# Attention and gate: products in four column strips instead of two row halves, scores in bursts

## The chip, the cores and the metric

One NeuronCore of a Trainium2 chip runs the whole kernel in one launch. The metric is the device time in microseconds. Its engines are TensorE (PE in the profile; PEld is its weight load), VectorE (DVE), ScalarE (ACT), GpSimd (POOL) and SyncE (SP), which issues most of the DMAs.

## The reference

x is 2048 x 640, one batch; attention has 32 heads of 20 columns; the dense layer has 1536 hidden columns. All inputs are float32.

```python
xn = _layernorm(x)                                # over the 640 columns
qkv = xn @ wqkv                                   # 640 x 1920
p = softmax(q @ k.T * 20 ** -0.5)                 # 32 heads, 2048 x 2048 each
s = (p @ v) @ wo
h = maximum(xn @ w1, 0)                           # 2048 x 1536
g = silu(h @ w2)
return x + s * g
```

## The kernel before

**Arithmetic.** The scores, the weighing of the values by the exponentials, and the dense products all run on TensorE. The dense ones ("products": projections of q, k and v, hidden layer, gate, output) are done with float16 pairs: each operand is split into a high and a low part, and a sum over k tiles of 128 rows has three terms a tile (`terms`: high by high, high by low, low by high). A product is 512 columns wide (q, k, hidden; 15 terms a sum) or 320 wide (values 15, gate 36, output 12 or 3 terms).

**Attention.** It walks 8 groups of 4 heads, 4 chunks of 512 queries and 16 tiles of 128 keys: 512 steps. For a step, four scores (`st`, line 732: keys by queries, 62 rows) go to ScalarE, which writes their exponentials to `pt` (line 736). Four more scores (`mx`, line 629: queries by keys, 60 rows) go to VectorE, which takes their maxima (line 633); these belong to a coming chunk and end up as rows subtracted inside the `st` scores. When a step's four exponentials are there, `weigh` (line 772) multiplies them with the values into the bank `pv`: four matmuls at once, each in a strip of 32 columns of the array (21 in use). They are float32 and stand in the profile as two matmuls each, eight a step.

**Forms of the array.** A score has at most 62 rows, so two scores run at once, one in each half of the rows (form "A", 64 rows by 128 columns). The values run in four strips (form "P", 128 rows by 32 columns). Transposes and some products run in the full array (form "F"). A product in `products` (line 314) runs in form "A": two sums at once, each with half of its rows, then the other halves, after the first ones are known to be done. At the start and for the last steps `whole` (line 328) does it in form "F".

**Banks.** Of eight PSUM banks one is `pv`; the other seven (`banks`) go round between scores, products and transposes. `take` gives the bank that comes free first; a bank is held until the engine that empties it is done.

**The order.** A planner in the program's own Python (class `Plan`, and the loop at the end) writes out the order of all instructions while the kernel is built; on the chip each engine does them in that order, with semaphores between engines. The planner keeps the time at which each engine comes free by fixed costs (MM 216 ns, MM_HALF 136, PAIR 220, PV 850, EXP 585, RED 605, SWITCH for a change of form). At each turn it takes the first that can be had: a pair of scores (`pair`: st with mx, or two of a kind) if its banks are free within STAY (60 ns) and the engine that gets it has less than SOON (560 ns) of work left, or less than FULL (1300 ns) if the array is in form "A" already; else weighing; else small transposes; else work of the start (`first`), else a step of the products (`fill`, kept from running too far ahead by `pace`). A step of a product is one term of the two sums' halves.

Of the kernel before, what the change touches and what calls it, by code (L numbers as in the profile page):

```python
# [17 lines left out]
P = 128  # L18
# [5 lines left out]
KD = D // P  # L24
KF = DFF // P
NT = S // P
CW = 512
# [21 lines left out]
EPS = 1e-5  # L49


SWITCH = 100
LAG = 210
BACK = 120
PAIR = 220
# [17 lines left out]
MIXED = 400  # L73
STOCK = 900
AHEAD = 40000
OTS = 4
FILLING = NT * 15 * MM_HALF * 2 + (KD - 1) * NC * 30 * MM + NC * KF * 15 * MM + NT * 72 * MM_HALF
LEAD = 80
# [79 lines left out]
def attention_gate(ctx: ExitStack, tc: tile.TileContext, x, wqkv, wo, w1, w2, out):  # L158
# [136 lines left out]
            res += [(ah[:, k, sa], bh[:, k, sb]), (ah[:, k, sa], bl[:, k, sb]), (al[:, k, sa], bh[:, k, sb])]  # L295
        return res

    def products(ps, pairs, free):

        if st_done[0] == 0 or st_done[0] > 4 * (STEPS - 10):
            return (yield from whole(ps, pairs, free))
        cost = MM if ps[0].shape[-1] == CW else MM_HALF
        half = [slice(0, P // 2), slice(P // 2, P)]
        n = len(pairs[0])
        for second in range(2):
            for i in range(n):
                yield free  # L310
                for which in range(2):
                    rows = half[which ^ second]
                    a, b = pairs[which][i]
                    nc.tensor.matmul(ps[which], a[rows], b[rows],  # L314
                                     start=(i == 0 and not second), stop=(i == n - 1 and bool(second)))
                got = plan.pe("A", cost, free)
            if not second:
                last = plan.issued
                yield from when(lambda: plan.seen > last)
        return got  # L320

    def whole(ps, pairs, free):

        cost = MM if ps[0].shape[-1] == CW else MM_HALF
        for which in range(2):
            for i, (a, b) in enumerate(pairs[which]):
                yield free
                nc.tensor.matmul(ps[which], a, b, start=(i == 0), stop=(i == len(pairs[which]) - 1))
                got = plan.pe("F", cost, free)
        return got  # L330

    def take_two():
        (a, fa), (b, fb) = take(), take()
# [131 lines left out]
    def qk(m, c):  # L465

        cs = slice(c * CW, (c + 1) * CW)
        sc = SQ / (SX * SW)
        yield from when(lambda: ("q", m) in pieces and ("k", m) in pieces and c in turned)
        ws, at = zip(*(pieces[name, m] for name in "qk"))  # L470
        bs, free = take_two()
        got = yield from products([banks[b] for b in bs], [terms(w, xt, KD, slice(0, P), cs) for w in ws],
                                  max(free, xt_ready[c], *at))
        for name, b in zip("qk", bs):
            hi = stage.tile([P, CW], F16, name=f"hi{name}{m}{c}", tag="hi")
            lo = stage.tile([P, CW], F16, name=f"lo{name}{m}{c}", tag="lo")
            nc.scalar.mul(hi, banks[b], sc)
            done = plan.op("act", 480, got)
            r = stage.tile([P, CW], F32, name=f"r{name}{m}{c}", tag="r", bufs=2)
            nc.scalar.mul(r, banks[b], sc)  # L480
            bank_free[b] = done = plan.op("act", 480, got)
            nc.gpsimd.tensor_sub(lo, r, hi)  # L482
            done = plan.op("pool", 1160, done)

            plan.at(done, lambda name=name, hi=hi, lo=lo: store(name, m, c, hi, lo))

    pack_ready = {}

# [97 lines left out]
    def v_tiles(n, t):  # L586

        yield from when(lambda: ("v", n) in pieces and t // TPC in turned)
        w, ready = pieces["v", n]
        bs, free = take_two()  # L590
        got = yield from products([banks[b][:, 0:HD] for b in bs],
                                  [terms(xt, w, KD, slice(u * P, (u + 1) * P), slice(0, HD)) for u in (t, t + 1)],
                                  max(free, ready, xt_ready[t // TPC]))
        for u, b in zip((t, t + 1), bs):
            nc.scalar.mul(va[n][:, u, :, 0:DH], banks[b][:, 0:HD].rearrange("p (h d) -> p h d", d=DH), v_scale[n])
            bank_free[b] = v_ready[n, u] = plan.op("act", 410, got)

# [246 lines left out]
    def gate_hidden():  # L846
# [34 lines left out]
        for f in range(KF):  # L881
            fs = slice(f * P, (f + 1) * P)
            yield from when(lambda: ("1", f) in pieces)
            w, ready = pieces["1", f]
            for pr in range(NC // 2):
                two = [slice(c * CW, (c + 1) * CW) for c in (2 * pr, 2 * pr + 1)]
                bs, free = take_two()
                got = yield from products([banks[b] for b in bs], [terms(w, xt, KD, slice(0, P), cs) for cs in two],
                                          max(free, ready))
                for c, cs, b in zip((2 * pr, 2 * pr + 1), two, bs):  # L890
                    r = stage.tile([P, CW], F32, name=f"hr{c}{f}", tag="r", bufs=2)
                    hi = stage.tile([P, CW], F16, name=f"hh{c}{f}", tag="hi")
                    lo = stage.tile([P, CW], F16, name=f"hl{c}{f}", tag="lo")
                    nc.scalar.activation(r, banks[b], AF.Relu, scale=SH / (SX * SW))  # L894
                    bank_free[b] = done = plan.op("act", 480, got)
                    nc.gpsimd.tensor_copy(hi, r)  # L896
                    plan.op("pool", 610, done)
                    nc.gpsimd.tensor_sub(lo, r, hi)  # L898
                    done = plan.op("pool", 1160)

                    def store(fs=fs, cs=cs, f=f, c=c, hi=hi, lo=lo):
                        nc.sync.dma_start(h_d["h"][fs, cs], hi)
                        nc.sync.dma_start(h_d["l"][fs, cs], lo)
                        h_stored[f, c] = plan.arrival(2 * 2 * P * CW, 2)

                    plan.at(done, store)
                if pr == 0 and f + 2 < KF:
                    piece("1", w1, f + 2, P)
        yield from when(lambda: all(("w2", n) in h_stored for n in range(KF))
# [7 lines left out]
    def gate_out():  # L917
# [46 lines left out]
        for c in range(S // HW):  # L964
# [3 lines left out]
            for u in range(HW // P):  # L968
                t = c * (HW // P) + u
                gt = gp.tile([P, D], F32, name=f"g{t}", tag="g")  # L970
                bs, free = take_two()
                got = yield from products([banks[b][:, 0:HD] for b in bs],
                                          [terms(ht, w2t, KF, slice(u * P, (u + 1) * P), ns) for ns in halves],
                                          max(free, ready))
                for n, (b, ns) in enumerate(zip(bs, halves)):
                    ps = banks[b][:, 0:HD]
                    th = gp.tile([P, HD], F32, name=f"th{t}{n}", tag="th")
                    nc.scalar.activation(th, ps, AF.Tanh, scale=cz)
                    done = plan.op("act", 420, got)
                    nc.vector.scalar_tensor_tensor(gt[:, ns], th, 1.0, ps, op0=ALU.add, op1=ALU.mult)  # L980
                    bank_free[b] = done = plan.op("dve", 430, done)

                def store(t=t, gt=gt):
                    nc.sync.dma_start(g_d[t * P:(t + 1) * P, :], gt)
                    g_stored[t] = plan.arrival(4 * P * D)

                plan.at(done, store)
        yield from when(lambda: len(g_stored) == NT and KD - 1 in wo_ready)
        st.close()
        cs_o = const.tile([P, 1], F32, name="cs_o")  # L990
# [28 lines left out]
    def out_first():  # L1019
# [16 lines left out]
        for t in range(NT):  # L1036
            if t + 1 < NT:
                os_[t + 1] = yield from transposed(t + 1, ots[t + 1], KL, landed[t + 1], "f")
            o, ready = os_.pop(t)
            bs, free = take_two()  # L1040
            got = yield from products([banks[b][:, 0:HD] for b in bs],
                                      [terms(o, wot, KL, slice(0, P), ns) for ns in halves],
                                      max(free, ready, out_state["ready"]))
            for b, ns in zip(bs, halves):
                ps = banks[b][:, 0:HD]
                nc.vector.scalar_tensor_tensor(gts[t][:, ns], ps, cs_o, gts[t][:, ns], op0=ALU.mult, op1=ALU.mult)  # L1046
                bank_free[b] = done = plan.op("dve", 550, max(got, landed[t]))
                nc.gpsimd.tensor_add(pre[:, t, ns], pre[:, t, ns], gts[t][:, ns])  # L1048
                plan.op("pool", 880, done)
            pre_done[0] = t + 1  # L1050
            if t + OTS < NT:
                yield from when(lambda: (NG - 2, (t + OTS) // TPC) in o_stored)
# [2 lines left out]
    def out_rest(c, on, ready):  # L1055
# [9 lines left out]
        for i in range(TPC):  # L1065
# [1 line left out]
            gt = gts[i]  # L1067
            ot = o[0][:, i:i + 1, :], o[1][:, i:i + 1, :]
            ws = [w[:, KL:KD, :] for w in wot]
            bs, free = take_two()  # L1070
            got = yield from whole([banks[b][:, 0:HD] for b in bs],
                                      [terms(ot, ws, 1, slice(0, P), ns) for ns in halves], max(free, ready))
            for n, (b, ns) in enumerate(zip(bs, halves)):
                ps = banks[b][:, 0:HD]
                nc.vector.scalar_tensor_tensor(gt[:, ns], ps, cs_o, gt[:, ns], op0=ALU.mult, op1=ALU.mult)  # L1075
                bank_free[b] = done = plan.op("dve", 550, max(got, landed))
                if n and c + 1 == NC:
# [2 lines left out]
                else:  # L1080
                    nc.gpsimd.tensor_add(gt[:, ns], gt[:, ns], pre[:, t, ns])
                    done = plan.op("pool", 880, done)
            plan.at(done, lambda t=t, gt=gt: nc.sync.dma_start(out[t * P:(t + 1) * P, :], gt))


    first = deque()
# [165 lines left out]
    while True:  # L1252
# [2 lines left out]
        go = plan.begin("A", 0)  # L1255
        options = choose(t)
        inside = plan.mode == "A"
        now = [o for o in options if o[0] <= go + STAY and o[1] < (FULL if inside else SOON)]
        if now:
            best = min(now, key=lambda o: (o[1] if len(set(o[2])) == 1 else o[1] - MIXED))  # L1260
            pair(best[2])
# [65 lines left out]
```

## Time and profile before

| what | value |
|---|---|
| time, median of 2 runs | 1789.01 us (1787.75 to 1790.27) |
| the profiled execution's own time | 1788.3 us |
| its span, from first to last instruction | 1786.5 us |
| mean granted clock of TensorE | 0.992 |
| busy: PE, DVE, ACT, POOL | 1734.0, 1451.6, 1390.6, 315.9 us |
| matmuls: in all, scores, values, products in halves | 14887, 4096, 4096, 5844 |

A row of the page's groups reads: line, engine, operation, what it writes and reads, shapes, count, then busy time, mean length of one in ns, and the idle time of the engine before these, with what ended most of it. A row of the timeline reads: start, length, engine, line, operation, and how many were merged into it. A row of busy times by stretch reads: the stretch, its length, then busy time and count for each engine that has any, the granted clock, the DMAs' share and GB/s. A matmul's listed length is its whole way through the array, while the next one follows closer; the distance between starts is what it costs.

### The profile page before, as it was taken

What the parts mean: (1) busy time and instruction counts of PE and PEld (TensorE: products, weight loads), DVE (VectorE), ACT (ScalarE), POOL (GpSimd) and SP (SyncE); (2) the same over time, 40 slices, a digit from 0 to 9 for tenths busy, and PEclk for the clock granted to TensorE, in tenths of its full rate; (3) what the DMA queues carried; (4) which work ended last, traced back from release to release, by engine and by line L of the source; (5) the groups of instructions that cost most, each with busy time, mean ns of one, the idle gap of its engine ahead of it and who ended that gap; (6) DMA issues with size and microseconds to landing.
All of it is one profiled execution on the core that took longest, in us unless ns stands there. A gap on an engine that the chain in (4) does not pass through costs nothing. (4 is left out here: it accounts for less than half of the span.)

```text
span 1786.5 us, 36686 instructions
## 1 busy us (share of the span) xinstructions
PE 1734.0 (97%) x14887; PEld 723.6 (41%) x14887; DVE 1451.6 (81%) x2512; ACT 1390.6 (78%) x2338; POOL 315.9 (18%) x338
## 2 busy tenths in 40 slices
PE   4999999999999999999999989999999999999998
PEld 3443334444332333444433324444444444344332
DVE  7699988888888888888888878888888888887522
ACT  3537788888888888887887868888788878887785
POOL 1631200002111455322221103000000000012221
PEclk8999999999999999999999999999999999999998
DMA  6324311201115332311112071131013100323332
GB/s 240 102 62 125 99 33 35 49 20 37 58 41 162 96 93 89 107 51 43 45 39 73 29 216 42 55 92 56 13 55 92 55 9 20 109 87 124 102 100 74
DMA packets 133995, 135.30 MB, mean 76 GB/s; under 512 B 26640, under 2 KB 110480, under 8 KB 133824
## 3 DMA queue, kind: packets, MB, share of 16 engines
q1 hardware_dynamic: 133248, 131.63, 24.4%
q8 instruction: 116, 1.90, 0.4%
q10 hardware_dynamic: 576, 1.31, 0.2%
q14 instruction: 55, 0.45, 0.1%
HBM read 85.32 MB, written 47.58 MB: 74 GB/s over the span
## 5 line engine op out<-in xcount | busy, mean ns | idle before, releaser
L736 ACT ACTIVATE pt<-ps,cexp 128x512 f32<-128x512 f32 x2048 | 1249.4, 689 | 293.0 <-PE ps L732 244.8
L633 DVE TENSOR_REDUCE m<-ps 128x1 f32<-128x512 f32 x2048 | 1274.4, 684 | 211.0 <-PE ps L629 204.6
L629 PE MATMUL ps<-kp,qp 60*128 60x512 f16 x2048 | 585.6, 378 | 5.3 <-ACT pt L736 3.7
L732 PE MATMUL ps<-qp,kp 62*128 62x512 f16 x2048 | 579.4, 379 | 9.3 <-DVE m L633 4.7
L772 PE MATMUL pv<-pt,va 128*21 128x512 f32 x4096 | 523.0, 600 | 0.0
L732 PEld LDWEIGHTS <-kp 62*128 62x128 f16 x2048 | 147.3, 93 | 332.2 <-issue 289.6
L629 PEld LDWEIGHTS <-qp 60*128 60x128 f16 x2048 | 150.1, 93 | 117.3 <-issue 84.7
L772 PEld LDWEIGHTS pv<-pt,va 128*21 128x21 f32 x4096 | 88.4, 100 | 237.3 <-issue 226.4
L1048 POOL TENSOR_TENSOR pre<-pre,go 128x320 f32<-128x320 f32 x32 | 27.0, 864 | 596.3 <-DVE go L1046 596.3
L314 PE MATMUL ps<-w2th,hh 64*128 64x320 f16 x768 | 126.5, 296 | 0.1
L314 PE MATMUL ps<-w2th,hl 64*128 64x320 f16 x768 | 126.0, 295 | 0.0
L314 PE MATMUL ps<-w2tl,hh 64*128 64x320 f16 x768 | 125.6, 295 | 0.0
L314 PEld LDWEIGHTS <-hh 64*128 64x128 f16 x1536 | 88.2, 94 | 51.2 <-issue 10.5
L314 PE MATMUL ps<-xt_hi,1h 64*128 64x512 f16 x480 | 102.7, 376 | 0.0
L314 PE MATMUL ps<-xt_lo,1h 64*128 64x512 f16 x480 | 102.1, 375 | 0.0
L314 PE MATMUL ps<-xt_hi,1l 64*128 64x512 f16 x480 | 100.3, 375 | 0.5 <-POOL 1l L287 0.5
L314 PEld LDWEIGHTS <-1h 64*128 64x128 f16 x960 | 58.7, 94 | 53.0 <-issue 18.7
L896 POOL CAST hh<-hr 128x512 f16<-128x512 f32 x48 | 29.3, 610 | 287.2 <-ACT hr L894 258.5
L482 POOL TENSOR_TENSOR loq<-rq,hiq 128x512 f16<-128x512 f32 x16 | 18.5, 1159 | 260.2 <-ACT rq L480 260.2
L314 PE MATMUL ps<-xt_hi,qh 64*128 64x512 f16 x150 | 56.4, 376 | 0.0
L314 PE MATMUL ps<-xt_lo,qh 64*128 64x512 f16 x150 | 56.4, 376 | 0.0
L898 POOL TENSOR_TENSOR hl<-hr,hh 128x512 f16<-128x512 f32 x48 | 55.7, 1160 | 3.8
(219 smaller groups left out, 1521.7 us busy)
## 6 DMA issues: line engine op xcount, KB each, us to landing
kp<-k_d SPq DMA_DIRECT2D x28, 240.0 KB
qp<-q_d SPq DMA_DIRECT2D x28, 240.0 KB
hh_d<-hh SPq DMA_DIRECT2D x48, 128.0 KB
hl_d<-hl SPq DMA_DIRECT2D x48, 128.0 KB
hh<-hh_d SPq DMA_DIRECT2D x8, 768.0 KB
hl<-hl_d SPq DMA_DIRECT2D x8, 768.0 KB
q_d<-hiq SPq DMA_DIRECT2D x20, 256.0 KB
k_d<-hik SPq DMA_DIRECT2D x20, 256.0 KB
```

The source lines that it names most:

```text
L314: nc.tensor.matmul(ps[which], a[rows], b[rows], start=(i == 0 and not second), stop=(i == n - 1 and bool(second)))
L482: nc.gpsimd.tensor_sub(lo, r, hi)
L629: nc.tensor.matmul(banks[b], qp[p % RING][r, t:t + P], kp[p % RING][r, kc * CW:(kc + 1) * CW], start=True, stop=True)
L633: nc.vector.tensor_reduce(m4[:, 2 * pr + j, qt, kc:kc + 1], banks[b], axis=AX.X, op=ALU.max)
L732: nc.tensor.matmul(banks[b], kp[p % RING][r, k * P:(k + 1) * P], qp[p % RING][r, c * CW:(c + 1) * CW], start=True, stop=True)
L736: exps[step, u] = nc.scalar.activation(pt[:, u, :], banks[b], AF.Exp, scale=cexp).ins
L772: nc.tensor.matmul(pv[32 * h:32 * h + DH + 1, :], va[g // 4][:, k, 4 * (g % 4) + h, :], pt[:, h, :], start=(k == 0), stop=(k == NT - 1))
L896: nc.gpsimd.tensor_copy(hi, r)
L898: nc.gpsimd.tensor_sub(lo, r, hi)
L1048: nc.gpsimd.tensor_add(pre[:, t, ns], pre[:, t, ns], gts[t][:, ns])
```

## The change

The products go to the values' form: each term of a sum is four matmuls, one for each strip of 32 columns of the stationary operand, with all 128 rows, into the 32 partitions of the strip in one bank. A sum takes one bank and is finished before the next one takes its own; what empties it (`after`) is issued right behind it. Only before the first score is the full array used. The rule by which a burst of scores may begin is another: outside of form "A" either GATHER (5) banks must be free, or one of ScalarE and VectorE must have less than URGENT (300 ns) of work left. SWITCH goes from 100 to 120. All callers hand their emptying work over as a function; one of them is shown.

```diff
-SWITCH = 100
+SWITCH = 120
+GATHER = 5
+URGENT = 300
...
-    def products(ps, pairs, free):
-        if st_done[0] == 0 or st_done[0] > 4 * (STEPS - 10):
-            return (yield from whole(ps, pairs, free))
-        cost = MM if ps[0].shape[-1] == CW else MM_HALF
-        half = [slice(0, P // 2), slice(P // 2, P)]
-        n = len(pairs[0])
-        for second in range(2):
-            for i in range(n):
-                yield free
-                for which in range(2):
-                    rows = half[which ^ second]
-                    a, b = pairs[which][i]
-                    nc.tensor.matmul(ps[which], a[rows], b[rows],
-                                     start=(i == 0 and not second), stop=(i == n - 1 and bool(second)))
-                got = plan.pe("A", cost, free)
-            if not second:
-                last = plan.issued
-                yield from when(lambda: plan.seen > last)
-        return got
...
+    def products(width, pairs, free, after, form="P"):
+        cost = MM if width == CW else MM_HALF
+        if st_done[0] == 0:
+            form = "F"
+        for which, terms_ in enumerate(pairs):
+            yield from when(lambda: soonest(1) < INF)
+            b, ready = take()
+            ready = max(ready, free)
+            ps = banks[b][:, 0:width]
+            n = len(terms_)
+            for i, (u, v) in enumerate(terms_):
+                yield ready
+                for j in range(0, P, P if form == "F" else 32):
+                    strip = slice(j, P if form == "F" else j + 32)
+                    nc.tensor.matmul(ps[strip], u[:, strip], v, start=(i == 0), stop=(i == n - 1))
+                got = plan.pe(form, cost, ready)
+            after(which, b, got)
...
-        bs, free = take_two()
-        got = yield from products([banks[b][:, 0:HD] for b in bs],
-                                  [terms(xt, w, KD, slice(u * P, (u + 1) * P), slice(0, HD)) for u in (t, t + 1)],
-                                  max(free, ready, xt_ready[t // TPC]))
-        for u, b in zip((t, t + 1), bs):
+        def after(which, b, got):
+            u = t + which
             nc.scalar.mul(va[n][:, u, :, 0:DH], banks[b][:, 0:HD].rearrange("p (h d) -> p h d", d=DH), v_scale[n])
             bank_free[b] = v_ready[n, u] = plan.op("act", 410, got)
+        yield from products(HD, [terms(xt, w, KD, slice(u * P, (u + 1) * P), slice(0, HD)) for u in (t, t + 1)],
+                            max(ready, xt_ready[t // TPC]), after)
...
-        now = [o for o in options if o[0] <= go + STAY and o[1] < (FULL if inside else SOON)]
+        gathered = inside or soonest(GATHER) <= go + STAY or min(plan.free["act"], plan.free["dve"]) - t < URGENT
+        now = [o for o in options if gathered and o[0] <= go + STAY and o[1] < (FULL if inside else SOON)]
```

More of the change, by code (lines that the diff above doesn't have):

```diff
@@ L296, in terms @@
         return res
-    def products(ps, pairs, free):
-        if st_done[0] == 0 or st_done[0] > 4 * (STEPS - 10):
-            return (yield from whole(ps, pairs, free))
-        cost = MM if ps[0].shape[-1] == CW else MM_HALF
-        half = [slice(0, P // 2), slice(P // 2, P)]
-        n = len(pairs[0])
-        for second in range(2):
-            for i in range(n):
-                yield free
-                for which in range(2):
-                    rows = half[which ^ second]
-                    a, b = pairs[which][i]
-                    nc.tensor.matmul(ps[which], a[rows], b[rows],
-                                     start=(i == 0 and not second), stop=(i == n - 1 and bool(second)))
-                got = plan.pe("A", cost, free)
-            if not second:
-                last = plan.issued
-                yield from when(lambda: plan.seen > last)
-        return got
[L322 to L330, printed above, removed]
+    def products(width, pairs, free, after, form="P"):
[15 more added lines that the diff above has]
+            after(which, b, got)
     def take_two():
@@ L470, in qk @@
         ws, at = zip(*(pieces[name, m] for name in "qk"))
-        bs, free = take_two()
-        got = yield from products([banks[b] for b in bs], [terms(w, xt, KD, slice(0, P), cs) for w in ws],
-                                  max(free, xt_ready[c], *at))
-        for name, b in zip("qk", bs):
+        def after(which, b, got):
+            name = "qk"[which]
             hi = stage.tile([P, CW], F16, name=f"hi{name}{m}{c}", tag="hi")
@@ L483, in qk @@
             done = plan.op("pool", 1160, done)
-            plan.at(done, lambda name=name, hi=hi, lo=lo: store(name, m, c, hi, lo))
+            plan.at(done, lambda: store(name, m, c, hi, lo))
+        yield from products(CW, [terms(w, xt, KD, slice(0, P), cs) for w in ws], max(xt_ready[c], *at), after)
     pack_ready = {}
@@ L589, in v_tiles, with after @@
         w, ready = pieces["v", n]
-        bs, free = take_two()
-        got = yield from products([banks[b][:, 0:HD] for b in bs],
-                                  [terms(xt, w, KD, slice(u * P, (u + 1) * P), slice(0, HD)) for u in (t, t + 1)],
-                                  max(free, ready, xt_ready[t // TPC]))
-        for u, b in zip((t, t + 1), bs):
+        def after(which, b, got):
+            u = t + which
             nc.scalar.mul(va[n][:, u, :, 0:DH], banks[b][:, 0:HD].rearrange("p (h d) -> p h d", d=DH), v_scale[n])
             bank_free[b] = v_ready[n, u] = plan.op("act", 410, got)
+        yield from products(HD, [terms(xt, w, KD, slice(u * P, (u + 1) * P), slice(0, HD)) for u in (t, t + 1)],
+                            max(ready, xt_ready[t // TPC]), after)
     mx_units = [(g, c, kc, qt, pr, j) for g in range(NG) for c in range(NC) for kc in range(NC)
@@ L886, in gate_hidden, with after @@
                 two = [slice(c * CW, (c + 1) * CW) for c in (2 * pr, 2 * pr + 1)]
[L887 to L890, printed above, removed]
+                def after(which, b, got):
+                    c, cs = 2 * pr + which, two[which]
                     r = stage.tile([P, CW], F32, name=f"hr{c}{f}", tag="r", bufs=2)
@@ L906, in gate_hidden @@
                     plan.at(done, store)
+                yield from products(CW, [terms(w, xt, KD, slice(0, P), cs) for cs in two], ready, after)
                 if pr == 0 and f + 2 < KF:
@@ L970, in gate_out, with after @@
                 gt = gp.tile([P, D], F32, name=f"g{t}", tag="g")
[L971 to L976, printed above, removed]
+                def after(n, b, got):
+                    ns, ps = halves[n], banks[b][:, 0:HD]
                     th = gp.tile([P, HD], F32, name=f"th{t}{n}", tag="th")
@@ L981, in gate_out @@
                     bank_free[b] = done = plan.op("dve", 430, done)
+                    if n:
+                        plan.at(done, store)
                 def store(t=t, gt=gt):
@@ L985, in store @@
                     g_stored[t] = plan.arrival(4 * P * D)
-                plan.at(done, store)
+                yield from products(HD, [terms(ht, w2t, KF, slice(u * P, (u + 1) * P), ns) for ns in halves],
+                                    ready, after)
         yield from when(lambda: len(g_stored) == NT and KD - 1 in wo_ready)
@@ L1039, in out_first, with after @@
             o, ready = os_.pop(t)
[L1040 to L1045, printed above, removed]
+            def after(n, b, got):
+                ns, ps = halves[n], banks[b][:, 0:HD]
                 nc.vector.scalar_tensor_tensor(gts[t][:, ns], ps, cs_o, gts[t][:, ns], op0=ALU.mult, op1=ALU.mult)
@@ L1049, in out_first @@
                 plan.op("pool", 880, done)
+            yield from products(HD, [terms(o, wot, KL, slice(0, P), ns) for ns in halves],
+                                max(ready, out_state["ready"]), after)
             pre_done[0] = t + 1
@@ L1069, in out_rest, with after @@
             ws = [w[:, KL:KD, :] for w in wot]
[L1070 to L1074, printed above, removed]
+            def after(n, b, got):
+                ns, ps = halves[n], banks[b][:, 0:HD]
                 nc.vector.scalar_tensor_tensor(gt[:, ns], ps, cs_o, gt[:, ns], op0=ALU.mult, op1=ALU.mult)
@@ L1082, in out_rest @@
                     done = plan.op("pool", 880, done)
-            plan.at(done, lambda t=t, gt=gt: nc.sync.dma_start(out[t * P:(t + 1) * P, :], gt))
+                if n:
+                    plan.at(done, lambda t=t, gt=gt: nc.sync.dma_start(out[t * P:(t + 1) * P, :], gt))
+            yield from products(HD, [terms(ot, ws, 1, slice(0, P), ns) for ns in halves], ready, after)
     first = deque()
```

## The prediction

> **What bounds it now.** I read the page first, then the busy time by stretches, then the timeline of TensorE inside one even stretch. From the page:
>
> ```profile
> span 1786.5 us, 36686 instructions
> PE 1734.0 (97%) x14887; PEld 723.6 (41%) x14887; DVE 1451.6 (81%) x2512; ACT 1390.6 (78%) x2338; POOL 315.9 (18%) x338
> PEclk8999999999999999999999999999999999999998
> ...
> L736 ACT ACTIVATE pt<-ps,cexp 128x512 f32<-128x512 f32 x2048 | 1249.4, 689 | 293.0 <-PE ps L732 244.8
> L633 DVE TENSOR_REDUCE m<-ps 128x1 f32<-128x512 f32 x2048 | 1274.4, 684 | 211.0 <-PE ps L629 204.6
> L629 PE MATMUL ps<-kp,qp 60*128 60x512 f16 x2048 | 585.6, 378 | 5.3 <-ACT pt L736 3.7
> L732 PE MATMUL ps<-qp,kp 62*128 62x512 f16 x2048 | 579.4, 379 | 9.3 <-DVE m L633 4.7
> L772 PE MATMUL pv<-pt,va 128*21 128x512 f32 x4096 | 523.0, 600 | 0.0
> ```
>
> TensorE is busy for 97% of the span at full clock and waits for nearly nothing, while ScalarE and VectorE, which empty its banks, idle mostly because a score is late (the releasers are L732 and L629). So TensorE bounds. Its busy share says little about how full it is, because pipelined matmuls overlap; the starts in the timeline do.
>
> ```profile
> 1204.00 1.91 PE L772 MATMUL pv<-pt,va 128*21 128x512 f32 x16
> 1205.85 0.39 PE L732 MATMUL ps<-qp,kp 62*128 62x512 f16 x2
> 1206.08 0.38 PE L629 MATMUL ps<-kp,qp 60*128 60x512 f16 x2
> 1206.39 1.06 PE L772 MATMUL pv<-pt,va 128*21 128x512 f32 x8
> 1207.38 0.39 PE L732 MATMUL ps<-qp,kp 62*128 62x512 f16 x1
> ...
> 1210.92 0.30 PE L314 MATMUL ps<-w2tl,hh 64*128 64x320 f16 x2
> 1211.06 0.30 PE L314 MATMUL ps<-w2th,hl 64*128 64x320 f16 x2
> 1211.19 0.30 PE L314 MATMUL ps<-w2th,hh 64*128 64x320 f16 x2
> ```
>
> This gives every price. Two weighing steps (16 matmuls) and the way out take 1.85 us, one step (8) and the way out 0.99 us, so a step is 0.86 us and the rest of 0.99, 0.13 us, is the change of form from four strips to two halves. A visit to the halves with two pairs of scores lasts 0.54 us (1205.85 to 1206.39); a pair is 0.22 to 0.23 us, so the way back costs some 0.10 us. **One visit between strips and halves costs 0.13 + 0.10 = 0.23 us.** A step of a product 320 wide takes 0.135 us (three starts in 0.27 us). One 512 wide takes 0.22 us:
>
> ```profile
> 407.60 0.38 PE L314 MATMUL ps<-xt_hi,kh 64*128 64x512 f16 x1
> 407.82 0.37 PE L314 MATMUL ps<-xt_lo,kh 64*128 64x512 f16 x1
> ```
>
> Now I fill one even stretch, 1200 to 1260 us. The busy time by stretch comes first for all instructions, then for lines 314, 772, 629 and 732 alone:
>
> ```profile
> 1200.00:1260.00 60.00, 60.00 (x614) 29.40 (x612) 53.10 (x93) 48.79 (x83) 0.00 (x0) 1.00 0.15 42
> 1200.00:1260.00 60.00, 31.41 (x306) 17.48 (x304) 1.00 0.15 42
> 1200.00:1260.00 60.00, 17.83 (x144) 3.14 (x144) 1.00 0.15 42
> 1200.00:1260.00 60.00, 22.52 (x80) 5.88 (x80) 1.00 0.15 42
> 1200.00:1260.00 60.00, 22.04 (x78) 5.86 (x78) 1.00 0.15 42
> ```
>
> Scores: 158 matmuls, 79 pairs, 79 x 0.22 = 17.4 us. Values: 144 / 8 = 18 steps, 15.5 us. Products: 306 / 2 = 153 steps, 20.7 us. Six others, about 1 us. Together 54.6. The timeline of the stretch has 12 runs of L772, the first at 1204.00 and the last at 1253.77:
>
> ```profile
> 1253.77 1.06 PE L772 MATMUL pv<-pt,va 128*21 128x512 f32 x8
> ```
>
> Twelve changes there and back are 2.8 us. What is left, **2.6 us in 60, is all that TensorE loses to waits for banks**. It is nearly full, and a change can only bring changes of form and those waits. Few changes are needed now because a product in halves has the scores' form: it stands between two pairs at no price, and only the values need another form.
>
> **The change part by part.** *Form of the products.* The counts:
>
> ```profile
> 0.00:1787.00 1787.00, 745.19 (x5844) 334.62 (x5844) 0.99 0.25 76
> L314 PE MATMUL ps<-w2th,hh 64*128 64x320 f16 x768 | 126.5, 296 | 0.1
> L314 PE MATMUL ps<-wo_h,oh 64*128 64x320 f16 x240 | 38.5, 298 | 0.1
> L314 PE MATMUL ps<-vh,xt_hi 64*128 64x320 f16 x160 | 28.4, 296 | 0.2 <-ACT pt L736 0.2
> ```
>
> Line 314 issues 5844. Each of the three narrow rows has two sisters of the same count, so 3 x (768 + 240 + 160) = 3504 are 320 wide and 2340 are 512 wide, in twos: 1752 and 1170 steps. A step does half the rows of two sums; afterwards one does all rows of one sum with four strips. The number of steps stays, 2922, and each streams the same columns, so at equal pace this term is 0. But a step now has four matmuls and four weight loads instead of two and two. Whether four go at the pace of two, the trace shows only for the values:
>
> ```profile
> 1206.39 0.14 PEld L772 LDWEIGHTS pv<-pt,va 128*21 128x21 f32 x8 [0.43 <-issue]
> ```
>
> Eight strip loads finish within 0.14 us from the instant at which the strip matmuls start, and those run on: four loads hide behind a pass of 0.43 us. Behind 0.135 us they just fit. Bounds: below, nothing (the stream sets the pace, and no row goes faster than its columns); above, the densest issue that the trace shows, 4 instructions in 0.135 us, would make 8 last 0.27 us, +0.135 x 1752 + 0.05 x 1170 = +295 us. I take 0, nearest to the values' row, whose strips start in one stroke.
>
> A rule speaks against it: the Trainium skill, "TensorE: Matmul & The Clock Gate", Part 3 ("What overlaps and what doesn't"), has weight loads overlap running matmuls only where the row group differs, and strips share all rows. The row above disagrees: these loads run beside matmuls on the same 128 rows. By the row the term is 0, by the rule it is the last rival below.
>
> *Changes of form.* Now each burst of scores is a visit, since products and values share a form. Before, the runs of L772 count 378 from the first to the last of these:
>
> ```profile
> 125.69 1.31 PE L772 MATMUL pv<-pt,va 128*21 128x512 f32 x8
> 1766.28 4.15 PE L772 MATMUL pv<-pt,va 128*21 128x512 f32 x16
> ```
>
> How many pairs will a burst have? Seven banks; a product holds one, and until ScalarE gets to its sum often a second. A burst begins when five banks are free, or when ScalarE or VectorE has under 300 ns left (URGENT), which comes first when both still hold a bank. Then four banks are free: two pairs. During these 0.44 us the two engines mostly free their two, and a third pair follows within STAY; a fourth needs banks of the first pair, whose exponential takes over 0.6 us, and the planner then takes a product and leaves the form. About three quarters of the bursts get three pairs, the others two: 2.7, so 2048 / 2.7 = 760 visits. Bounds: 683 with three always, 1024 with two. **(760 - 378) x 0.23 = +88 us.** Transposes and other full-array runs change form as before, 0.
>
> *Waits.* 2.6 us per 60 over the even part (120 to 1620 us, 1500 us) is 65 us; they come from pairs that the order put ahead of products while their banks were not yet free, and from the second half of a product that had to be held back until the first was seen done. Gathering waits for banks in strips, where there is always a product to do, so most go: I let a quarter stay, **-49 us** (bounds 0 and -65). What is late next is the third pair of a burst. Ahead of 240 us, where the order is looser, I add **-10 us** (0 to -25).
>
> *ScalarE and VectorE.* The first score of a visit reaches its engine late:
>
> ```profile
> 1206.27 1.26 ACT L736 ACTIVATE pt<-ps,cexp 128x512 f32<-128x512 f32 x2 [2.04 <-PE ps L732]
> ```
>
> From 1205.85 to 1206.27 is 0.42 us. If an engine had run dry at each visit, VectorE would need 1452 + 760 x 0.42 = 1771 us: just under TensorE's sum. I take 0 on top, but this cover is thin (the second rival).
>
> *Small edits.* One bank a sum: the first of two sums is emptied one sum earlier, and ScalarE, POOL and SP get the same instructions and stores in the same order; 0. The new wait is for one bank where it was for two; behind it stands the whole queue of TensorE, and it is shorter. The last products at line 328 go from full array to strips, 0.
>
> **Sum.** The profiled execution took 1788.3 us, 0.7 below the median 1789.01, so it stands for it. 1788.3 + 88 - 49 - 10 = **1817 us**.
>
> **Rivals.** *Long bursts.* If the planner finds six banks nearly always and sometimes a fourth pair, 640 visits cost +60, all waits go (-65) and the head gives its 25: 1758; with 683 visits 1768. For it: VectorE idles 211 us, so banks are often free. Against: URGENT starts bursts with four banks. About 1765 us.
>
> *Short bursts.* Place: the start rule of a burst; price: 0.23 us a visit. If URGENT fires while the product holds two banks, bursts have two pairs: (1024 - 378) x 0.23 = +149, less 59 in waits, 1878 us. VectorE says the same: 1452 + 1024 x 0.42 = 1882. It passes the forecast's upper end below 2.3 pairs a burst. Here the change also misses what it says, bursts of three. About 1880 us.
>
> *Strips short of instructions.* Eight instructions in 0.135 us is twice the densest rate in the trace. It decides from 17 ns an instruction; at 25 ns a narrow step lasts 0.20 us, +0.065 x 1752 = 114 us, about 1930 us. For it: no row shows that rate sustained. Against: strips of the values start in one stroke, and scores and values, with few instructions per us, let the queue fill.
>
> *Loads not hidden.* If strip loads could not run beside matmuls, each step would add one load of 0.10 us (the eight of the load row, started in one stroke, take 0.14): 2922 x 0.10 = +292, 2109 us. The load row speaks against it. The rule of the Trainium skill named above would do this.
>
> **How the numbers follow.** Forecast 0.52, its own range 1795 to 1845; long bursts 0.20 (1740 to 1790); short bursts 0.15 (1850 to 1900); short of instructions 0.10; loads 0.03. The range takes the upper part of the long bursts and the short ones' middle: 1760 to 1892, leaving out some 0.06 below and 0.14 above. About 2% is what a measurement of this kernel can tell from no change, here 1753 to 1825. Faster: 0.10, all from long bursts. Same: the other 0.10 of these and 0.36 of the forecast, 0.46. Slower: 0.16 of the forecast and the last three, 0.44.
>
> **What would show it.** The timeline should have runs of scores of two and three pairs, some 26 to 30 in 60 us instead of 12, products and values in one run between them, product steps of four 32-column matmuls still 0.135 and 0.22 us apart. PEld waits for "issue" before L732 and L629 should grow with the visits. If narrow steps stand 0.2 us apart, the third rival holds; if VectorE's idle time before L633 grows past 300 us at unchanged steps, the second. I would be wrong on the faster side if TensorE's waits now are more than the 2.6 us in 60 that my sum leaves, for then the strips give back more than the visits cost.

## The result and the profile after

The changed kernel takes 1818.22 us (1817.81 to 1818.63, two runs) against 1789.01: a ratio of 1.0163, 95% interval 1.0139 to 1.0188, slower by 1.6% and clear of the noise. The forecast was 1817. Its profiled span is 1816.8 us. From the page of the changed kernel, and its line 317 (products), alone over the span:

```profile
span 1816.8 us, 49101 instructions
PE 1757.6 (97%) x21091; PEld 614.9 (34%) x21091; DVE 1468.5 (81%) x2508; ACT 1407.6 (77%) x2343; POOL 317.7 (17%) x337
PEclk8999999999999999999999999999999999999999
...
L624 DVE TENSOR_REDUCE m<-ps 128x1 f32<-128x512 f32 x2048 | 1292.1, 684 | 240.8 <-PE ps L620 233.2
L727 ACT ACTIVATE pt<-ps,cexp 128x512 f32<-128x512 f32 x2048 | 1259.9, 687 | 272.4 <-PE ps L620 153.4
```

```profile
0.00:1817.00 1817.00, 689.54 (x12438) 305.31 (x12438) 0.99 0.25 75
```

TensorE still bounds: 97% busy at a granted clock of 0.99. Of the two emptying engines VectorE idles a little more than before ahead of its maxima (241 us after 211) and ScalarE a little less ahead of its exponentials (272 after 293). Products are now 12438 matmuls, and this costs no pace. The timeline of TensorE shows 320-wide steps of four strips, then 512-wide ones:

```profile
1212.36 0.31 PE L317 MATMUL ps<-w2tl,hh 128*32 128x320 f16 x4
1212.50 0.31 PE L317 MATMUL ps<-w2th,hl 128*32 128x320 f16 x4
1212.63 0.31 PE L317 MATMUL ps<-w2th,hh 128*32 128x320 f16 x4
1212.77 0.31 PE L317 MATMUL ps<-w2tl,hh 128*32 128x320 f16 x4
1212.90 1.03 PE L763 MATMUL pv<-pt,va 128*21 128x512 f32 x8
1213.87 0.39 PE L723 MATMUL ps<-qp,kp 62*128 62x512 f16 x1
```

```profile
452.29 0.39 PE L317 MATMUL ps<-xt_hi,kh 128*32 128x512 f16 x4
452.51 0.39 PE L317 MATMUL ps<-xt_lo,kh 128*32 128x512 f16 x4
452.72 0.39 PE L317 MATMUL ps<-xt_hi,kl 128*32 128x512 f16 x4
452.94 1.03 PE L763 MATMUL pv<-pt,va 128*21 128x512 f32 x8
453.90 0.39 PE L620 MATMUL ps<-kp,qp 60*128 60x512 f16 x2
454.13 0.38 PE L723 MATMUL ps<-qp,kp 62*128 62x512 f16 x2
454.35 0.41 PE L620 MATMUL ps<-kp,qp 60*128 60x512 f16 x2
454.69 0.40 PE L317 MATMUL ps<-xt_hi,qh 128*32 128x512 f16 x4
```

Steps stand 0.135 and 0.215 us apart, as in halves. From the last product to the values there is no gap (0.13 us after 1212.77, a step's own length): the adjacency that the change makes is real. The price stands at the scores. A weighing step and the way out take 0.96 us (452.94 to 453.90), 0.10 more than the step; three pairs and the way back take 0.79 us (453.90 to 454.69), 0.12 to 0.13 more than three times 0.22. Between 1200 and 1260 us there are 29 runs of scores, where the values alone made 12 visits to strips before.

### The profile page after: what moved, and what is told of

Its sections match the earlier page's. It is cut to its first block, busy times and chain, and to the rows that moved or that the text cites. A ratio compares the mean times of both kernels' runs of the same rounds, so it can differ in the third digit from the quotient of the medians.

```text
span 1816.8 us, 49101 instructions
## 1 busy us (share of the span) xinstructions
PE 1757.6 (97%) x21091; PEld 614.9 (34%) x21091; DVE 1468.5 (81%) x2508; ACT 1407.6 (77%) x2343; POOL 317.7 (17%) x337
## 5 line engine op out<-in xcount | busy, mean ns | idle before, releaser
L624 DVE TENSOR_REDUCE m<-ps 128x1 f32<-128x512 f32 x2048 | 1292.1, 684 | 240.8 <-PE ps L620 233.2
L727 ACT ACTIVATE pt<-ps,cexp 128x512 f32<-128x512 f32 x2048 | 1259.9, 687 | 272.4 <-PE ps L620 153.4
L723 PE MATMUL ps<-qp,kp 62*128 62x512 f16 x2048 | 503.3, 381 | 7.6 <-ACT pt L727 3.4
L620 PE MATMUL ps<-kp,qp 60*128 60x512 f16 x2048 | 503.4, 381 | 1.9 <-DVE m L624 0.9
L317 PE MATMUL ps<-w2th,hl 128*32 128x320 f16 x1536 | 119.8, 301 | 1.4 <-DMA hl<-hl_d 1.4
L317 PE MATMUL ps<-w2th,hh 128*32 128x320 f16 x1536 | 120.2, 301 | 0.1
L317 PE MATMUL ps<-w2tl,hh 128*32 128x320 f16 x1536 | 120.2, 301 | 0.0
L317 PEld LDWEIGHTS <-hh 128*32 128x32 f16 x3072 | 77.1, 96 | 79.3 <-issue 65.2
L317 PE MATMUL ps<-xt_lo,1h 128*32 128x512 f16 x960 | 94.5, 383 | 0.0
L317 PE MATMUL ps<-xt_hi,1h 128*32 128x512 f16 x960 | 94.5, 382 | 0.0
L317 PE MATMUL ps<-xt_hi,1l 128*32 128x512 f16 x960 | 94.2, 381 | 0.0
L317 PE MATMUL ps<-vh,xt_hi 128*32 128x320 f16 (+1 forms) x400 | 49.3, 301 | 3.3 <-ACT vh L281 2.5
```

What stands on the lines that cost most here:

```text
L317: nc.tensor.matmul(ps[strip], u[:, strip], v, start=(i == 0), stop=(i == n - 1))
L620: nc.tensor.matmul(banks[b], qp[p % RING][r, t:t + P], kp[p % RING][r, kc * CW:(kc + 1) * CW], start=True, stop=True)
L624: nc.vector.tensor_reduce(m4[:, 2 * pr + j, qt, kc:kc + 1], banks[b], axis=AX.X, op=ALU.max)
L723: nc.tensor.matmul(banks[b], kp[p % RING][r, k * P:(k + 1) * P], qp[p % RING][r, c * CW:(c + 1) * CW], start=True, stop=True)
L727: exps[step, u] = nc.scalar.activation(pt[:, u, :], banks[b], AF.Exp, scale=cexp).ins
```

## The experiments

Each kernel was timed beside runs of the kernel before on the same chip (1789.3 to 1789.5 us there); the changed kernel's 1818.22 us is the time above, measured beside 1789.01. Visits and changes of form are those of the order written into the kernel. A visit is one run in the scores' form; the changed kernel has 850 and 1827 changes of form, the kernel before 512 runs with 1059 changes.

**Strips alone, the old start rule.**

```diff
-        gathered = inside or soonest(GATHER) <= go + STAY or min(...) - t < URGENT
+        gathered = True
```

> The changed kernel with the old rule for starting a burst (no gathering): products in strips alone. Its order has 1011 visits to the scores' form (changed kernel 850, before 378 from the values and 512 runs of scores in all). Theory of visits (time is TensorE's work plus 0.2 us a visit, strips at full pace): +161 x 0.21 = +34 us, less a few us of waits, about 1845 us. Rival, gathering costs more than it saves because the engines run dry: no gathering would give about 1800 us or less. Rival, strips are slow and visits are nearly free: the time stays at 1818 us.

Measured 1849.09 us, ratio 1.0337 (1.0322 to 1.0352), 30.9 us above the changed kernel. The number is the expected one, but it is not the price of 161 visits. In the profile of this order (a run of 1853.6 us) the last score starts at 1627 us, in the changed kernel's at 1789, so products stand alone at the end, and from 1690 us on TensorE waits 19 us there for VectorE's emptying and for loads (changed kernel 1 us). By the starts, all changes between halves and strips together, waits ahead of bursts included, take only 18 us more (213 against 195). So the expectation came out by luck. What stands is that strips without gathering cost 60 us, the end included, and with it 29: gathering is not what costs.

**Bursts alone, products in halves.**

```diff
-SWITCH = 100
+SWITCH = 120
...
+GATHER = 5
+URGENT = 300
...
+        gathered = inside or soonest(GATHER) <= go + STAY or min(...) - t < URGENT
-        now = [o for o in options if o[0] <= go + STAY and ...]
+        now = [o for o in options if gathered and o[0] <= go + STAY and ...]
```

> The kernel before with the new rule for starting a burst and SWITCH 120, products in halves as they were. Its order has 1030 changes of form where the kernel before has 1059. Theory of visits: nearly no change, 1785 to 1800 us (-29 x 0.1 us, and a few us more waits). Rival, gathering itself starves ScalarE and VectorE: 1810 us or more, that is most of the +29 us is the rule's and not the strips'.

Measured 1793.12 us, ratio 1.0022 (1.0012 to 1.0031). Without strips the rule costs 4 us. It changes the order little there: 497 runs in the halves' form instead of 512.

**Full array in place of strips.**

```diff
-        if st_done[0] == 0:
-            form = "F"
+        form = "F"
```

> The changed kernel with every product in the full array instead of four strips: one matmul and one weight load a step of the same columns. Then products and values no longer share a form: 2110 changes of form where the changed kernel has 1827. Theory of visits: +283 x 0.1 = +28 us, about 1846 us. Rival, four strips issue too slowly (each step with eight instructions longer than 0.135 or 0.22 us): full array would be faster than the changed kernel, below 1810 us.

Measured 1851.41 us, ratio 1.0346 (1.0331 to 1.0362), 33 us above the changed kernel for 283 more changes of form. Here too some 10 us are waits at the end (11 us from 1690 us on, 1 in the changed kernel), so a change costs nearer 0.08 us than 0.12 by this sum. The steps stand 0.135 and 0.215 us apart as before: four strips are not slower than one full array, and what they save is the changes of form that a shared form makes unnecessary.

**Bursts of at most two pairs.**

```diff
+        burst[0] *= inside
-        now = [o for o in options if gathered and ...]
+        now = [o for o in options if gathered and burst[0] < 2 and ...]
...
             pair(best[2])
+            burst[0] += 1
...
+        burst[0] = 0
```

> The changed kernel with bursts held to two pairs. Its order has 1065 visits instead of 850. Theory of visits: +215 x 0.21 = +45 us, less up to 19 us of waits that the planner drops, 1844 us (1835 to 1863). Rival, visits are nearly free and time hangs on how soon the engines are fed: 1800 to 1818 us.

Measured 1843.55 us, ratio 1.0303 (1.0286 to 1.032). Ten of the 1065 runs are longer than two pairs, because the counter starts again whenever the planner waits. Of the +45 for 215 visits 25 are left. The experiment after the next shows why.

**Without waits for banks.** The same edit in both kernels, each in its own order:

```diff
-            exps[step, u] = nc.scalar.activation(pt[:, u, :], banks[b], AF.Exp, ...)
+            exps[step, u] = nc.scalar.activation(pt[:, u, 0:64], banks[b][:, 0:64], AF.Exp, ...)
-            nc.vector.tensor_reduce(..., banks[b], axis=AX.X, op=ALU.max)
+            nc.vector.tensor_reduce(..., banks[b][:, 0:64], axis=AX.X, op=ALU.max)
...
+        for t in ring:
+            nc.gpsimd.memset(t, 1.0)
```

> The kernel before in its own order, but ScalarE's exponential and VectorE's maximum read only 64 of the 512 columns of a score (the other weights stay 1), so that hardly a bank is late. What is taken away is the waiting for banks. Theory of visits: the kernel before loses 60 to 90 us to these waits, so 1700 to 1730 us. Rival, its waits are few (under 20 us): above 1770 us.

> The changed kernel in its own order with the same short reads of 64 columns. Theory of visits: without waits for banks the whole price of the visits stands alone: 850 visits of strips and halves where the kernel before has 377, times 0.2 to 0.23 us, so 85 to 110 us above the same experiment on the kernel before; about 1795 to 1810 us in itself. Rival, the +29 us are waits of a new kind (a third pair whose banks are late): it would come down to the time of the same experiment on the kernel before, within 20 us.

Measured 1708.56 us (before) and 1765.81 us (changed). The kernel before loses 1789.35 - 1708.56 = 81 us to waits for the two engines, the changed one 1818.22 - 1765.81 = 52. (Short reads free the banks early and also give the exponentials and maxima early; the edit does not tell the two apart.) So 28 us of waits came back, and the rest of the change costs 57 us, less than the 85 to 110 that I expected. In the changed kernel's experiment the engines have plenty of room:

```profile
PE 1713.8 (97%) x21091; PEld 586.4 (33%) x21091; DVE 598.6 (34%) x2508; ACT 680.0 (39%) x2343; POOL 323.0 (18%) x340
```

VectorE and ScalarE work for 34% and 39% of the time, TensorE is busy for 97% as ever: what is left is its own work and its changes of form. I counted the starts in both of these traces, each against its stream, the time between starts when nothing intervenes (216 ns for 512 columns, 136 for 320, 429 for a float32 pass of the values):

| us | before, no waits | changed, no waits | difference |
|---|---|---|---|
| changes between halves and strips | 85 (721) | 167 (1552) | +82 |
| changes to and from the full array | 61 | 53 | -8 |
| over the stream inside a run of one form | 46 | 26 | -20 |
| steps of scores, values, products | 1373 | 1389 | +16 |
| matmuls within full-array runs | 120 | 107 | -13 |

The last two are the same work: the last products went from full array to strips. The sum is +57. The two halves drift apart inside a run, so the split between the first and the third row is not sharp: if a run counts as ended with its last pair, the kernel before has 90 and 41 us there, at the same sum.

**Two pairs, without waits.** Both edits together, to see the price of a visit by itself.

> Bursts held to two pairs (1065 visits instead of 850) together with the short reads of 64 of 512 columns by ScalarE and VectorE, so that the price of a visit stands without waits. The changed kernel with short reads took 1765.8 us, the kernel before 1708.6, 57 apart, less than the 85 to 110 expected. Theory A, a visit costs 0.20 us as the timeline says, and the strips and the gathering give some 25 to 30 us back elsewhere on TensorE (steps in halves and pairs follow each other less closely than strips): +215 x 0.20 = +43, 1809 us. Theory B, a visit costs only 57 us / 415 more visits = 0.14 us and there is nothing else: +30, 1795 us.

Measured 1831.31 us (1826.88 to 1833.9): 65.5 above the changed kernel's experiment, beyond both theories, so as a sum it decides nothing. By the starts, changes between halves and strips rose from 1552 to 1994 and from 167 to 211 us: 44 us for 442, 0.20 a visit, as theory A has it. Some 20 us are new and lie at the end. Waits of TensorE from 1690 us on (who waited for whom: us in total, times, longest):

```profile
PE ps L317 <- DVE gr L1065: 9.9, 3, 5.0
PE ps L1003 <- DMA ot<-o_d: 7.7, 2, 4.4
```

Here the scores are through early (the last starts at 1705 us of 1829; in the changed kernel's experiment at 1737 of 1765), and the products that they outran stand alone at the end, where nothing covers their loads and emptying. Two pairs with whole reads take 1843.55 us, so in that order only 12 us are waits for the two engines: against 52 in the changed kernel 40 came back, which is why the fourth experiment stayed below +45 in spite of this end.

**Only the maxima short.**

> The changed kernel where only VectorE's maximum reads 64 of 512 columns; ScalarE's exponential is whole. With both short the time was 1765.8 us, so 52 us of waits for banks stay in the changed kernel. If VectorE holds the banks that are late (it is the fuller of the two), 30 us or more go: below 1790 us. If ScalarE holds them, under 15 us go: above 1803 us. If a burst's pair needs both, about half: 1790 to 1803 us.

Measured 1807.9 us, 10 of the 52 us. Freeing VectorE alone does little. The starts say where: counting a burst as late when its first pair starts over 0.15 us after the stream of the strips has ended (0.11 is usual), 103 of the changed kernel's bursts are late, by 23 us in all beyond the usual. With only the maxima short it is 118 and 25 us, with both short 8 and 4 us. So the wait ahead of a burst does not need VectorE; it points to ScalarE. ScalarE's reads alone were not made short.

**Not urgent.**

```diff
-URGENT = 300
+URGENT = 0
```

> The changed kernel with URGENT 0 instead of 300: a burst waits for five free banks until an engine is dry. Its order has 814 visits instead of 850. Theory of visits alone: -36 x 0.21 = -8 us, 1810 us. Theory with the thin cover (each visit leaves ScalarE or VectorE dry for up to 0.4 us, and they are nearly full): slower by some 0.1 us a visit or more, 1880 us (1850 to 1900).

Measured 1870.52 us, ratio 1.0452 (1.0438 to 1.0467): 36 visits fewer and 52 us more. The idle time ahead of the maxima and the exponentials, from the groups of this kernel:

```profile
L624 DVE TENSOR_REDUCE m<-ps 128x1 f32<-128x512 f32 x2048 | 1286.6, 683 | 300.2 <-PE ps L620 292.5 <-PE ps L723 1.8
L727 ACT ACTIVATE pt<-ps,cexp 128x512 f32<-128x512 f32 x2048 | 1262.2, 688 | 342.5 <-PE ps L620 192.6 <-PE ps L723 144.6
```

240.8 became 300.2 us, 272.4 became 342.5. This growth, 59 and 70 us, is no proof that dry engines cost the time: with the same work in a span that is 52 us longer, idle time must grow by about as much. The starts show it at TensorE: 181 bursts are late instead of 103, by 51 us instead of 23, and pairs inside a burst lose 34 us over their stream instead of 23, together some 38 of the 52. So the time fits the theory with the thin cover, but what is shown is that bursts begin later and still wait for their first pair. Why was not tried.

**A version that beats both.** Products in halves, and a single weighing step held back for a second one unless both engines have over 900 ns of work:

```diff
-SWITCH = 100
+SWITCH = 120
-AHEAD = 40000
+AHEAD = 60000
...
-        if n and (coming == INF or min(...) - t > STOCK or plan.mode != "A"):
+        full = n == 2 or n and where(pv_done[0])[2] == NT - 1 or coming == INF or min(...) - t > 900
+        if n and full and (coming == INF or min(...) - t > STOCK or plan.mode != "A"):
```

> The kernel before with products in halves; SWITCH 120, AHEAD 60000, and a single weighing step is held back for a second one unless both engines have over 900 ns of work left. Its order has 1053 changes of form (kernel before 1059) and some 12 us less idle time in the planner's own account. Theory of visits and waits: 1789 - 12 = 1777 us (1770 to 1787). Rival, the planner's idle time does not tell the real waits: 1785 to 1795 us.

Measured 1780.63 us, ratio 0.995 (0.9937 to 0.9964). A small gain at nearly the same number of changes, so it must come from somewhere else, and fewer waits are the likely place; the three edits were not tried one by one.

## Why the prediction was right, and where its sum was not

The time came out within 2 us and the direction was right, for the cause that was named: changes of form. That it came so close is luck: two terms missed by about 30 us each and cancelled. The signs came as described: 29 runs of scores in 60 us, steps at their old pace, weight loads idle longer ahead of the scores (506 us instead of 374), VectorE's idle time ahead of its maxima under 300 us.

*Pace of the strips: right.* 0 was taken, and the timeline shows 0.135 and 0.215 us for four strips. Both rivals on it are gone: 8 instructions go in 0.135 us, 17 ns each. (The prediction called this twice the densest rate in its trace, but its own row of eight loads, with the matmuls that start beside them, was denser for one stroke; open was only whether such a rate lasts.) And the loads hide, since they start with the matmuls and run beside them:

```profile
1205.98 0.24 PEld L317 LDWEIGHTS <-hh 128*32 128x32 f16 x8
1206.25 0.11 PEld L317 LDWEIGHTS <-hl 128*32 128x32 f16 x4
```

Eight loads, of two steps, begin within the steps ahead of their own, on the same 128 rows; a load exposed in every step would have shown as steps 0.23 us apart. The Trainium skill ("TensorE: Matmul & The Clock Gate", Part 3, "What overlaps and what doesn't") has this overlap only for different row groups; neither the values' nor the products' strips here bear that out.

*Changes of form: right in sum, off in its parts.* +88 us was predicted, +82 measured without waits. The visits were 850, not 760, because a burst had 2.4 pairs and not 2.7: 453 had three, 266 two, and 123 a single pair, which the prediction did not count on. Some of these runs begin or end at the full array, so there were 831 more changes between halves and strips, 415 round trips and not 850 - 378 = 472. And the price was 0.20 us, not 0.23: the 0.13 us read for the way out (0.99 us for values that come right behind scores) held some 0.03 us that values behind a product do not take (0.96 us above). These errors are the small ones.

*Waits: the failed step.* I let 59 us come back; 28 did. The base was rather too small (I put 65 to the even part, and the kernel before loses 81 in all), but 52 us stay instead of 16. "Most go" was wrong. By the starts, in the changed kernel the way from strips into a burst takes 113 us and without waits 91, pairs inside a burst 23 over the stream and without waits 11. So the first pair waits most, and not the third, which the prediction had named as the next to be late. Why is open: that a burst begins on URGENT with just enough banks is not shown, and with URGENT 0 these waits grew.

*A gain not in the sum.* Some 28 us, the second and third rows of the table: runs of strips follow their stream more closely than halves mixed with scores, and there are fewer changes to and from the full array (275 instead of 338), a term that the prediction put at 0. Where the halves lose their 20 us was not tried.

*The rivals.* Long bursts (640 to 683 visits) did not come. Short bursts were the nearer one: 850 lies between 760 and 1024, and the experiment with two pairs shows that even 1065 visits make 1844 and not 1880. A visit costs 0.20 us and not 0.23, 69 of the 81 us of waits come back instead of 59, and the gain above is in none of the rivals' sums; the waits at the end take some of it away. VectorE does not reach its limit there: it is busy for 81% of the span.

## What to carry to other kernels

On an engine that is full, price a reordering by the changes of form that it adds, each read from the starts in the timeline: it was 0.1 us a change here, and 831 changes were 82 us. Work in a shared form stood free beside its neighbour here, so it pays to share the form of the neighbour that comes most often: the scores (2048 pairs), not the values (512 steps). And the waits of a full engine are measured, not guessed, by making the others' work short: 81 and 52 us here, where I had 65 and 16. Last, before a difference between two orders is divided by a count, look at their ends: in four experiments here 10 to 20 us were waits of products that stood alone there.

## What the runs showed of the hardware

Four 32-column strips with their own loads go at the pace of one full array or two halves, within 0.005 us a step, at 320 columns (0.135 us) and at 512 (0.215 us), through the whole kernel. A change between halves and strips cost 0.10 to 0.11 us in either direction (1552 of them for 167 us), whether values or products stood on the strips' side. The first step of products behind a change lasts 0.01 us longer than the ones that follow (0.146 and 0.226 us).
